# Later transposes of the query numerators, earlier transposes of h, and a last output product in two column parts

## Chip, cores and metric

The kernel runs on one core of one Trainium2 chip. The metric is the device time in microseconds of one execution; lower is better. TensorE (PE, with its weight loads as PEld), VectorE (DVE), ScalarE (ACT), GpSimd (POOL) and SyncE (SP, which here only issues DMAs) each run their own instruction stream in order and wait for one another through semaphores.

## What is computed

The input x has 2048 tokens of 448 features. Both branches start from its layer norm and share one output:

```python
xn = layernorm(x)
# A: linear attention, 16 heads of 28; phi(t) = [softmax(t), softmax(-t)] over 28 features
q, k, v = split(xn @ wqkv)
pq, pk = q @ w_phi, k @ w_phi                      # per head
kv = phi(pk).T @ v ;  z = phi(pk).sum(tokens)      # per head
o  = (phi(pq) @ kv) / (phi(pq) @ z + 1e-6)
A  = o @ wo
# B: token shift and MLP
h  = gelu(layernorm(xn) @ w1)                      # quarters of h shifted by +1,-1,+2,-2 tokens
x1 = xn + shift(h) @ w2
B  = x1 + gelu(layernorm(x1) @ w3) @ w4            # w3: 448 -> 1792, w4: 1792 -> 448
out = x + A + B
```

## The kernel before

Tokens are cut into 16 tiles of 128, in four groups g of four tiles. A small recorder (`Recorder`) takes every operation in program order, finds its hazards by byte ranges, and gives each engine its own in-order stream with the waits that are needed. So the place of a call in the program sets its place in its engine's stream, and nothing else reorders work. All compute calls go through one-line helpers, which is why the profile shows few line numbers: L188 is every matmul, L192 every PE transpose, L196 every activation, L200 every elementwise operation, L203 every DMA transpose, L206 every plain DMA. Tiles of one region show under the region's name or that of its first user: `phik` also holds the MLP's activations h3T, `vaug` also the scratch and output tiles of the late part, `xnT` also o_tok and oT, `w` stands for w1 to w4, `hi` for eqT.

The steps that the change and the prediction touch:

- `q_pair(i, b)`: two tiles of xn @ (wq w_phi) in two PSUM banks; ACT writes exp(+) and exp(-) of them to `eq_tok`, a ring of eight tiles in the region `eq`.
- `eq_T(i)`, in the plan `E`: two DMA transposes on SP of that tile into `eqT`, a ring of eight tiles that fills the region `hi` (16 KB a partition).
- `num_tile(i, b0)`, `N`: 16 matmuls with `eqT` of tile i as weights against `kvq`, then a chain of six operations on DVE (the normaliser) and two on POOL that write `o_tok`. `o_T(i)`, `O`, transposes that by one DMA on SP into `oT`.
- `chunks(n, b)`: 2 of the 56 chunks of x1n @ w3 (14 for each group, 512 tokens wide), with gelu on ACT into h3T. `batch` puts two or more of such pairs together.
- `fin_full(i)`, `Ff`: 14 matmuls with h3T against w4 and 3 with oT against wo, 448 columns each, in one bank; `fin_tail(i)` adds a last half-height matmul; `fin_out(i)` adds x + xn (`x_sum`, on POOL) on DVE into `outb`; `store(i)`, `St`, sends the tile out on SP. For tiles 14 and 15 `fin_full` does all of its four wo matmuls.
- `h_T(i)`: one DMA transpose on SP of a tile of h into hT. `w2_mul(i, b)` needs hT of tiles i-1 to i+1; with `w2_add` (x1 and its statistics, on DVE) it is `W`.
- `ln_scale` on POOL turns the statistics of four tiles of x1 into scales; `g_apply` and `g_T` (`ga`) normalise x1 and transpose it on SP into gT for the chunks of a group.
- `k_norm(i)`: sums and reciprocals on DVE, then a multiplication on POOL (the last tile's on DVE) that normalises phi(pk) in `phik`. `kv_tile(i)`: eight small matmuls with it; after tile 15, `kv_copy` on DVE, `kv_blocks` (8 PE transposes, then DVE) give `kvq`.

Up to tile 3 of `kv_tile` the program is written out; then a list `plan` of nine rows drives it. Each row names the banks of its chunk pairs, which form a batch, and the steps after them in order:

```python
for *heads, steps in plan:
    pairs_b = [chunks(n + 2 * k, b) for k, b in enumerate(heads)]
    n += 2 * len(pairs_b)
    batch(pairs_b[:2], pairs_b[2:], led=held)
    held = [step[1] for step in steps if step[0] is fin_full]
    for step in steps:
        step[0](*step[1:])
```

After the plan come tiles 12 and 13's ends and the last two output products, of tiles 14 and 15.

Of the kernel before, what the change touches and what calls it, by code (L numbers as in the profile page):

```python
# [5 lines left out]
ACT = mybir.ActivationFunctionType  # L6
ALU = mybir.AluOpType
# [201 lines left out]
def bass_parallel_sum__linear_kernel_hedgehog__mixer_s_mlp__prompt_kernel(  # L209
    nc, A_x, A_wqkv, A_w_phi, A_wo, B_x, B_w1, B_w2, B_w3, B_w4, out,  # L210
):
    _, S, D = A_x.shape
# [3 lines left out]
    NT, NG, KC, NC, NM, FC, HP = 16, 4, 4, 4, 4, 14, 32  # L216
    CR = 112
    SHIFTS = [1, -1, 2, -2]
    QE = DH + 2
    PAD = 16  # L220
    HW = S + 2 * PAD
    x2d, out2d = A_x[0], out[0]

    es = ExitStack()
    with es:
        R = Recorder(nc, es)
# [9 lines left out]
        def view(h, cols, dt=BF16, at=0):  # L236
            a = h[:, at // 2:at // 2 + cols * DTB[dt] // 2]
            return a if dt == BF16 else a.bitcast(dt)
# [5 lines left out]
        for b in range(4):  # L244
            t = es.enter_context(nc.psum_tensor("bank%d%d" % (2 * b, 2 * b + 1), [128, 1024], F32))
            R.track(t, 4096, psum=True)
            pairs.append(t)
        banks = [pairs[b // 2][:, 512 * (b % 2):512 * (b % 2) + 512] for b in range(8)]
# [11 lines left out]
        vaug = view(vaug_r, NT * 512).rearrange("p (t c) -> p t c", t=NT)  # L260
        gT = new("gT", 2 * KC * 512).rearrange("p (b c s) -> p b c s", b=2, c=KC)
        eq_r = region("eq", 8 * 2 * 512 * 2)
        eq_tok = view(eq_r, 8 * 2 * 512).rearrange("p (t s d) -> p t s d", t=8, s=2)
        hi_r = region("hi", NC * 2 * 1024 * 2)
        eqT = view(hi_r, 8 * 2 * 512).rearrange("p (t s c f) -> p t s c f", t=8, s=2, c=NC)
        wT = view(hi_r, 2 * NC * 512).rearrange("p (t c d) -> p t c d", t=2, c=NC)
        wv_r = region("wv", KC * D * 2)
        wv = view(wv_r, KC * D).rearrange("p (c d) -> p c d", c=KC)
# [6 lines left out]
        wo = new("wo", KC * D).rearrange("p (c d) -> p c d", c=KC)  # L275
        w3 = new("w3", KC * F).rearrange("p (c f) -> p c f", c=KC)
        w4_r = region("w4", FC * D * 2)
        w4 = view(w4_r, FC * D).rearrange("p (c d) -> p c d", c=FC)
# [12 lines left out]
        mv2 = new("mv2", NT * 8, F32).rearrange("p (t c) -> p t c", t=NT)  # L291
        rs2 = new("rs2", NT * 8, F32).rearrange("p (t c) -> p t c", t=NT)
# [27 lines left out]
        dve, pool = "DVE", "POOL"  # L320
# [97 lines left out]
        def ln_scale(mvt, rst, a, n, neg):  # L418
            R.ew(pool, "tensor_scalar", mvt[:, a:a + n, 2], mvt[:, a:a + n, 1], LN_EPS, 1.0, op0=ALU.add, op1=ALU.mult)
            R.ew(pool, "tensor_tensor", rst[:, a:a + n, 0], mvt[:, a:a + n, 2], mhalf[:, 0:n], op=ALU.pow)  # L420
            if neg:
                R.ew(pool, "tensor_scalar", rst[:, a:a + neg, 1], mvt[:, a:a + neg, 0], -1.0, 0.0, op0=ALU.mult,
                     op1=ALU.add)
# [92 lines left out]

        def q_pair(i, b):
            def out():
                for s in range(2):
                    R.act(eq_tok[:, i % 8:i % 8 + 2, s, :].rearrange("p t (c d) -> p t c d", c=NC)[:, :, :, 0:CR],  # L520
                          two(b)[:, :, 0:D].rearrange("p t (c d) -> p t c d", c=NC), ACT.Exp, scale=1.0 - 2.0 * s)
            return [tok(wpq, i, b), tok(wpq, i + 1, b + 1)], out

        def eq_T(i):
            for s in range(2):
                R.dma_t(eqT[:, i % 8, s, :, :], eq_tok[:, i % 8, s, :])

        def batch(last, first=(), between=(), led=()):
            for p, _ in last:
# [21 lines left out]
        def h_T(i):  # L551
            R.dma_t(hT[:, :, PAD + 128 * i:PAD + 128 * i + 128], h_tok[i])

        def k_norm(i, eng=pool):
            for j in (i, i + 1):
                ph = phik[:, j, :, :].rearrange("p s (h e) -> p (s h) e", e=DH)
                r = j % 4
                R.ew(dve, "tensor_reduce", ksum[:, r, :], ph, axis=AX.X, op=ALU.add)
                R.ew(dve, "reciprocal", rks[:, r, :], ksum[:, r, :])
                R.ew(eng if j % 2 else pool, "tensor_tensor", ph, ph, rks[:, r, :].unsqueeze(2).to_broadcast([128, 2 * H, DH]),  # L560
                     op=ALU.mult)
# [29 lines left out]
        def w2_tile(i, b):  # L591
            w2_mul(i, b)
            w2_add(i, b)
# [23 lines left out]
        def num_tile(i, b0):  # L617
            g, j = divmod(i, 4)
            r = i % 2
            bs = [banks[b0], banks[b0 + 1]]  # L620
            for s in range(2):
                for c in range(NC):
                    R.mm(bs[s][:, 4 * QE * c:4 * QE * c + 4 * QE], eqT[0:CR, i % 8, s, c, :],
                         kvq[0:CR, 2 * c + s, :], True, True)
            pp, pm = (b[:, 0:H * QE].rearrange("p (h e) -> p h e", e=QE) for b in bs)
            rcpm, rho, dsum, rden = (q_s[:, r, 16 * k:16 * k + 16] for k in range(4))
            R.ew(dve, "reciprocal", rcpm, pm[:, :, DH + 1])
            R.ew(dve, "tensor_tensor", rho, pp[:, :, DH + 1], rcpm, op=ALU.mult)
            R.ew(dve, "tensor_tensor", q_t[:, r, :, :], pm[:, :, 0:DH + 1],
                 rho.unsqueeze(2).to_broadcast([128, H, DH + 1]), op=ALU.mult)  # L630
            R.ew(dve, "tensor_tensor", q_n[:, r, :, :], pp[:, :, 0:DH + 1], q_t[:, r, :, :], op=ALU.add)
            R.ew(dve, "scalar_tensor_tensor", dsum, pp[:, :, DH + 1], DEN_EPS, q_n[:, r, :, DH],
                 op0=ALU.mult, op1=ALU.add)
            R.ew(dve, "reciprocal", rden, dsum)

            cut = 10 if i % 2 else 7
            for h0, h1, at in ((0, cut, 0), (cut - 1, H, 64)):
                R.ew(pool, "tensor_tensor",
                     o_tok[:, i % 4, DH * h0 + at:DH * h1 + at].rearrange("p (h e) -> p h e", e=DH),
                     q_n[:, r, h0:h1, 0:DH], rden[:, h0:h1].unsqueeze(2).to_broadcast([128, h1 - h0, DH]), op=ALU.mult)  # L640
            if i >= NT - 2:
                c0 = 192 + 64 * (i % 2)
                R.ew(pool, "memset", o_tok[:, i % 4, c0:c0 + 64], 0.0)
# [16 lines left out]
        def x_sum(i):  # L660
            R.ew(pool, "tensor_tensor", xs[:, i % 2, :], xn[:, i, 0:D], xtok[:, i, :], op=ALU.add)

        def fin_bank(i):
            return (0 if i > 13 else 4) + i % 2

        def fin_full(i):
            g, j = divmod(i, 4)
            b = banks[fin_bank(i)]
            x_sum(i)
            for fc in range(FC):  # L670
                R.mm(b[:, 0:D], h3T[:, g % 2, fc, 128 * j:128 * j + 128], w4[:, fc, :], fc == 0, False)
            for kc in (0, 3, 2 - i % 2, 1 + i % 2) if i >= NT - 2 else (0, 3, 2 - i % 2):
                R.mm(b[:, 0:D], oT[:, g % 2, kc, 128 * j:128 * j + 128], wo[:, kc, :], False, kc == 1 + i % 2)

        def fin_tail(i):
            g, j = divmod(i, 4)
# [148 lines left out]
        w2_tile(5, 7)  # L825
        qs(4)
        h_T(11)
        for i in range(4, 8):
            eq_T(i)
        k_norm(8)  # L830
        w2_tile(6, 6)
        ks(12)
        w2_tile(7, 7)
        k_norm(10)
        k_norm(12)
        ln_scale(mv2, rs2, 4, 4, 4)
        k_norm(14, dve)
        table("gelu_apprx_tanh_and_others")
        for i in range(4):
# [10 lines left out]
                g_apply(4 * g + j, eng)  # L850
                g_T(4 * g + j)

        def hts():
            for i in range(12, 16):
                h_T(i)
            load_lap(wo, A_wo)

        def sc(g):
# [9 lines left out]
        def stats2(i):  # L868
# [1 line left out]

        plan = [
            (0, 2, 6, [(kv, 4, 8), (load_w4,)]),
            (0, 2, 6, [(table, "exp_and_others"), (ga, 1, dve), (hts,), (qq, 8), (kv, 8, 16), (kv_copy,), (W, 8, 6),
                       (qq, 12), (table, "gelu_apprx_tanh_and_others"), (kv_blocks, 5), (w2_mul, 9, 7), (w2_mul, 10, 6),
                       (w2_add, 9, 7, False), (N, 0, 4), (O, 0), (w2_add, 10, 6, False), (stats2, 9), (stats2, 10), (E, 8)]),
            (0, 2, 4, 6, [(N, 1, 0), (O, 1), (E, 9), (Ff, 0), (W, 11, 3), (sc, 2), (N, 2, 0), (O, 2), (N, 3, 6), (O, 3),
                          (Ff, 1)]),
            (0, 2, 6, [(Ff, 2), (St, 0), (ga, 2), (W, 12, 2), (N, 4, 0), (O, 4), (N, 5, 6), (O, 5), (E, 10), (W, 13, 3), (Ff, 3),
                       (St, 1), (E, 11), (E, 12), (E, 13)]),
            (0, 2, 6, [(Ff, 4), (St, 2), (W, 14, 2), (W, 15, 3), (sc, 3), (N, 6, 0), (O, 6), (N, 7, 6), (O, 7),  # L880
                       (Ff, 5), (St, 3), (ga, 3)]),
            (0, 2, 6, [(Ff, 6), (St, 4), (N, 8, 0), (O, 8), (N, 9, 6), (O, 9), (E, 14), (Ff, 7), (St, 5), (E, 15)]),
            (0, 2, 6, [(Ff, 8), (St, 6), (N, 10, 0), (O, 10), (N, 11, 6), (O, 11), (Ff, 9), (St, 7)]),
            (0, 2, 6, [(Ff, 10), (St, 8), (N, 12, 0), (O, 12), (N, 13, 6), (O, 13), (Ff, 11), (St, 9)]),
            (0, 2, 6, [(N, 14, 0), (O, 14), (Ff, 12), (St, 10), (N, 15, 2), (O, 15), (Ff, 13), (St, 11)])]
        held = []
        n = 0
# [13 lines left out]
        fin_full(14)  # L901
        fin_out(14)
        store(14)
        fin_full(15)
        for h in range(2):
            c = slice(224 * h, 224 * h + 224)
            R.ew(dve, "tensor_tensor", outb[:, 3, c], banks[fin_bank(15)][:, c], xs[:, 1, c], op=ALU.add)
            R.dma(out2d[128 * 15:, c], outb[:, 3, c], "ACT" if h else "SP")

        R.emit()  # L910

# [27 lines left out]
```

## Time and profile before

| | us |
|---|---|
| median of 3 runs | 182.85 (182.31, 182.85, 183.42) |
| the profiled execution, whole | 182.53 |
| its span, first to last instruction | 180.8 |
| PE busy in the span | 175.3 |
| DVE busy | 117.6 |
| POOL busy | 94.6 |
| ACT busy | 80.2 |

The granted TensorE clock was full throughout. Rows of a profile read as follows. In the timeline: start, duration, engine, source line, operation, output<-inputs, partitions x elements, count, and in brackets the idle time of that engine just before and who ended it; several like instructions in a row are merged. In a group: busy time, then the mean duration of one in ns, then idle time before it. A row for SPq or ACTq is an engine's queue issuing a DMA, not the transfer; a DMA group's last number is the median from issue to landing.

### The profile page before, as it was taken

What the parts mean: (1) busy time and instruction counts of PE and PEld (TensorE: products, weight loads), DVE (VectorE), ACT (ScalarE), POOL (GpSimd) and SP (SyncE); (2) the same over time, 40 slices, a digit from 0 to 9 for tenths busy, and PEclk for the clock granted to TensorE, in tenths of its full rate; (3) what the DMA queues carried; (4) which work ended last, traced back from release to release, by engine and by line L of the source; (5) the groups of instructions that cost most, each with busy time, mean ns of one, the idle gap of its engine ahead of it and who ended that gap; (6) DMA issues with size and microseconds to landing.
All of it is one profiled execution on the core that took longest, in us unless ns stands there. A gap on an engine that the chain in (4) does not pass through costs nothing.

```text
span 180.8 us, 3146 instructions
## 1 busy us (share of the span) xinstructions
PE 175.3 (97%) x1200; PEld 88.4 (49%) x1200; DVE 117.6 (65%) x269; ACT 80.2 (44%) x99; POOL 94.6 (52%) x144
## 2 busy tenths in 40 slices
PE   7799999999999999999999999999999999999993
PEld 5454655454445435454553644553644644635551
DVE  5898679659999996874595196195282352654621
ACT  2378881799999639677104104203306006024000
POOL 6874582068999599002457626037835063151650
PEclk9999999999999999999999999999999999999999
DMA  5996445499565499684643323555543422030231
GB/s 165 346 220 128 90 89 102 82 337 232 104 74 110 93 276 229 126 107 70 179 87 62 88 57 64 115 82 112 112 94 80 100 67 80 0 62 25 54 112 44
DMA packets 59142, 21.04 MB, mean 116 GB/s; under 512 B 50872, under 2 KB 58616, under 8 KB 59128
## 3 DMA queue, kind: packets, MB, share of 16 engines
q1 hardware_dynamic: 55656, 16.55, 44.5%
q10 hardware_dynamic: 3472, 4.30, 7.8%
q8 instruction: 9, 0.15, 0.4%
q14 instruction: 5, 0.04, 0.1%
HBM read 7.08 MB, written 1.84 MB: 49 GB/s over the span
## 4 chain that ended last, share of the span: by engine, by line
PE 74%; DVE 16%; POOL 6%; issue 2%; ACT 0%; DVEq 0%
PE bank L188 72%; DVE ksum L200 6%; POOL phik L200 5%; DVE st L200 3%; DVE xn L200 2%; PE bank L192 2%; DVE vaug L200 2%; DVE rks L200 1%; POOL rs L200 1%; POOL mv L200 1%; DVE wpq L200 1%; DVE mv L200 1%; ACT xnT L196 0%; DVEq L166 0%; DVE gT L200 0%
## 5 line engine op out<-in xcount | busy, mean ns | idle before, releaser
L196 ACT ACTIVATE phik<-bank 128x1024 bf16<-128x1024 f32 (+1 forms) x44 | 40.2, 990 | 68.1 <-PE bank L188 68.0
L188 PE MATMUL bank<-gT,w 128*128 128x512 bf16 (+1 forms) x224 | 46.1, 379 | 0.1
L188 PE MATMUL bank<-w,phik 128*128 128x448 bf16 x224 | 45.0, 352 | 0.0
L200 DVE TENSOR_TENSOR vaug<-bank,vaug 128x464 f32<-128x464 f32 (+3 forms) x65 | 33.0, 514 | 17.8 <-PE bank L188 13.9
L200 POOL TENSOR_TENSOR xnT<-vaug 128x196 bf16<-128x196 f32 (+1 forms) x32 | 18.1, 586 | 48.1 <-DVE vaug L200 48.1
L188 PEld LDWEIGHTS bank<-w,phik 128*128 128x128 bf16 x224 | 21.5, 98 | 19.3 <-issue 0.2
L188 PEld LDWEIGHTS bank<-gT,w 128*128 128x128 bf16 (+1 forms) x224 | 17.9, 97 | 24.0 <-issue 5.1
L200 POOL TENSOR_TENSOR phik<-phik,rks 128x896 bf16<-128x896 bf16 x15 | 25.0, 1697 | 3.1 <-DVE rks L200 3.0
L200 POOL TENSOR_TENSOR vaug<-xn,xtok 128x448 f32<-128x448 bf16 x16 | 16.4, 1031 | 1.4 <-DVE vaug L200 1.4
L200 DVE TENSOR_TENSOR xn<-bank,xn 128x448 bf16<-128x448 f32 x16 | 9.4, 599 | 11.8 <-PE bank L188 11.7
L200 DVE TENSOR_REDUCE ksum<-phik 128x32 f32<-128x896 bf16 x16 | 16.6, 1036 | 0.0
L200 DVE RECIPROCAL vaug<-bank 128x16 f32<-128x16 f32 x16 | 3.7, 228 | 17.8 <-PE bank L188 17.8
L188 PE MATMUL bank<-wo,xnT 128*128 128x448 bf16 (+1 forms) x64 | 14.5, 354 | 0.1
L200 POOL TENSOR_TENSOR rs<-mv,mhalf 128x2 f32<-128x2 f32 (+1 forms) x16 | 13.8, 865 | 1.3
L188 PE MATMUL bank<-w,hT 112*128 112x448 bf16 x64 | 14.3, 352 | 0.0
L196 ACT ACTIVATE eq<-bank 128x896 bf16<-128x896 f32 x16 | 13.4, 922 | 1.9 <-PE bank L188 1.9
L188 PE MATMUL bank<-wv,xnT 128*128 128x448 bf16 (+1 forms) x64 | 14.0, 354 | 0.1
L188 PE MATMUL bank<-w,xnT 128*128 128x448 bf16 (+1 forms) x64 | 13.9, 352 | 0.0
L188 PE MATMUL bank<-wpk,xnT 128*128 128x448 bf16 (+1 forms) x64 | 12.2, 353 | 0.0
L188 PE MATMUL bank<-wpq,xnT 128*128 128x448 bf16 (+1 forms) x64 | 12.1, 353 | 0.0
L200 POOL TENSOR_SCALAR mv<-mv 128x4 f32<-128x4 f32 x4 | 1.6, 406 | 17.8 <-DVE mv L200 17.7
L200 DVE BATCH_NORM_STATS2 st<-xn 128x6 f32<-128x448 bf16 x16 | 9.9, 620 | 0.4
(65 smaller groups left out, 173.9 us busy)
## 6 DMA issues: line engine op xcount, KB each, us to landing
w<-in_B_w_dram ACTq DMA_DIRECT2D x2, 896.0 KB, 6.5
out_dram<-vaug SPq DMA_DIRECT2D x15, 112.0 KB, 1.9
w<-in_B_w_dram ACTq DMA_DIRECT2D x1, 1568.0 KB, 9.3
xtok<-in_A_x_dram SPq DMA_DIRECT2D x2, 448.0 KB, 6.6
hi<-eq SPq DMA_TRANSPOSE x32, 2.5
wo<-in_A_wo_dram SPq DMA_DIRECT2D x2, 224.0 KB, 2.9
w<-in_B_w_dram SPq DMA_DIRECT2D x1, 392.0 KB, 4.3
xtok<-in_A_x_dram SPq DMA_DIRECT2D x3, 112.0 KB, 2.6
```

Source lines behind the costliest of these rows:

```text
L188: self.op("PE", lambda e: e.matmul(out, lhsT, rhs, start=start, stop=stop, skip_group_check=True), [out], [lhsT, rhs])
L192: self.op("PE", lambda e: e.transpose(out, in_, ident), [out], [in_, ident])
L196: self.op("ACT", lambda e: e.activation(out, in_, func, **kw), [out], [in_] + aps)
L200: self.op(eng, lambda e: getattr(e, name)(out, *args, **kw), [out], aps)
```

## The change

The eight-slot `eqT` becomes a ring of four, in the lower half of `hi`. The upper half goes to `eq_tok`, which becomes a ring of twelve. `eq_T(i + 4)` now follows `num_tile(i)` in the plan, since it overwrites the slot that `num_tile(i)` has read; before, tiles 4 to 7 were transposed ahead of the plan, and tiles 8 to 15 at other places of it. `h_T` of tiles 12 to 15 moves from the plan's second row to a place ahead of the plan. In that second row the w2 product of tile 8 moves ahead of the kv products of tiles 8 to 15. `ln_scale` for tiles 4 to 7 moves ahead of `k_norm(10)`. The output product of tile 15 is done as 256 columns in one bank and then 192 in another, each with its own addition and store, where before one product of 448 columns was followed by two additions and stores of 224.

```diff
-        eq_tok = view(eq_r, 8 * 2 * 512).rearrange("p (t s d) -> p t s d", t=8, s=2)
-        eqT = view(hi_r, 8 * 2 * 512).rearrange("p (t s c f) -> p t s c f", t=8, s=2, c=NC)
+        eqT = view(hi_r, 4 * 2 * 512).rearrange("p (t s c f) -> p t s c f", t=4, s=2, c=NC)
+        eq_tok = [view(r, 1024, at=at + 2048 * k).rearrange("p (s d) -> p s d", s=2)
+                  for r, at, n in ((eq_r, 0, 8), (hi_r, 8192, 4)) for k in range(n)]
...
         def eq_T(i):
             for s in range(2):
-                R.dma_t(eqT[:, i % 8, s, :, :], eq_tok[:, i % 8, s, :])
+                R.dma_t(eqT[:, i % 4, s, :, :], eq_tok[i % 12][:, s, :])
...
+        def product(i, b, c):
+            g, j = divmod(i, 4)
+            s = slice(128 * j, 128 * j + 128)
+            o = b[:, 0:c.stop - c.start]
+            for fc in range(FC):
+                R.mm(o, h3T[:, g % 2, fc, s], w4[:, fc, c], fc == 0, False)
+            for kc in (0, 3, 2 - i % 2, 1 + i % 2) if i >= NT - 2 else (0, 3, 2 - i % 2):
+                R.mm(o, oT[:, g % 2, kc, s], wo[:, kc, c], False, kc == 1 + i % 2)
+
         def fin_full(i):
...
+            product(i, banks[fin_bank(i)], slice(0, D))
...
         h_T(11)
-        for i in range(4, 8):
-            eq_T(i)
         k_norm(8)
         w2_tile(6, 6)
         ks(12)
         w2_tile(7, 7)
+        ln_scale(mv2, rs2, 4, 4, 4)
         k_norm(10)
+        for i in range(12, 16):
+            h_T(i)
         k_norm(12)
-        ln_scale(mv2, rs2, 4, 4, 4)
         k_norm(14, dve)
...
-        def hts():
-            for i in range(12, 16):
-                h_T(i)
+        def load_wo():
             load_lap(wo, A_wo)
...
         plan = [
             (0, 2, 6, [(kv, 4, 8), (load_w4,)]),
-            (0, 2, 6, [(table, "exp_and_others"), (ga, 1, dve), (hts,), (qq, 8), (kv, 8, 16), (kv_copy,), (W, 8, 6),
+            (0, 2, 6, [(table, "exp_and_others"), (ga, 1, dve), (load_wo,), (qq, 8), (W, 8, 6), (kv, 8, 16), (kv_copy,),
                        (qq, 12), (table, "gelu_apprx_tanh_and_others"), (kv_blocks, 5), (w2_mul, 9, 7), (w2_mul, 10, 6),
-                       (w2_add, 9, 7, False), (N, 0, 4), (O, 0), (w2_add, 10, 6, False), (stats2, 9), (stats2, 10), (E, 8)]),
-            (0, 2, 4, 6, [(N, 1, 0), (O, 1), (E, 9), (Ff, 0), (W, 11, 3), (sc, 2), (N, 2, 0), (O, 2), (N, 3, 6), (O, 3),
+                       (w2_add, 9, 7, False), (N, 0, 4), (E, 4), (O, 0), (w2_add, 10, 6, False), (stats2, 9), (stats2, 10),
+                      ]),
+            (0, 2, 4, 6, [(N, 1, 0), (E, 5), (O, 1), (Ff, 0), (W, 11, 3), (sc, 2), (N, 2, 0), (E, 6), (O, 2), (N, 3, 6), (E, 7), (O, 3),
                           (Ff, 1)]),
-            (0, 2, 6, [(Ff, 2), (St, 0), (ga, 2), (W, 12, 2), (N, 4, 0), (O, 4), (N, 5, 6), (O, 5), (E, 10), (W, 13, 3), (Ff, 3),
-                       (St, 1), (E, 11), (E, 12), (E, 13)]),
-            (0, 2, 6, [(Ff, 4), (St, 2), (W, 14, 2), (W, 15, 3), (sc, 3), (N, 6, 0), (O, 6), (N, 7, 6), (O, 7),
+            (0, 2, 6, [(Ff, 2), (St, 0), (ga, 2), (W, 12, 2), (N, 4, 0), (E, 8), (O, 4), (N, 5, 6), (E, 9), (O, 5), (W, 13, 3), (Ff, 3),
+                       (St, 1),]),
+            (0, 2, 6, [(Ff, 4), (St, 2), (W, 14, 2), (W, 15, 3), (sc, 3), (N, 6, 0), (E, 10), (O, 6), (N, 7, 6), (E, 11), (O, 7),
                        (Ff, 5), (St, 3), (ga, 3)]),
-            (0, 2, 6, [(Ff, 6), (St, 4), (N, 8, 0), (O, 8), (N, 9, 6), (O, 9), (E, 14), (Ff, 7), (St, 5), (E, 15)]),
-            (0, 2, 6, [(Ff, 8), (St, 6), (N, 10, 0), (O, 10), (N, 11, 6), (O, 11), (Ff, 9), (St, 7)]),
+            (0, 2, 6, [(Ff, 6), (St, 4), (N, 8, 0), (E, 12), (O, 8), (N, 9, 6), (E, 13), (O, 9), (Ff, 7), (St, 5),]),
+            (0, 2, 6, [(Ff, 8), (St, 6), (N, 10, 0), (E, 14), (O, 10), (N, 11, 6), (E, 15), (O, 11), (Ff, 9), (St, 7)]),
...
-        fin_full(15)
-        for h in range(2):
-            c = slice(224 * h, 224 * h + 224)
-            R.ew(dve, "tensor_tensor", outb[:, 3, c], banks[fin_bank(15)][:, c], xs[:, 1, c], op=ALU.add)
-            R.dma(out2d[128 * 15:, c], outb[:, 3, c], "ACT" if h else "SP")
+        x_sum(15)
+        for c, b, e in ((slice(0, 256), 1, "SP"), (slice(256, D), 2, "ACT")):
+            product(15, banks[b], c)
+            R.ew(dve, "tensor_tensor", outb[:, 3, c], banks[b][:, 0:c.stop - c.start], xs[:, 1, c], op=ALU.add)
+            R.dma(out2d[128 * 15:, c], outb[:, 3, c], e)
```

More of the change, by code (lines that the diff above doesn't have):

```diff
@@ L518, in out @@
             def out():
+                r, at = (eq_r, i % 12) if i % 12 < 8 else (hi_r, 4 + i % 12 - 8)
+                e = view(r, 2048, at=2048 * at).rearrange("p (t s c d) -> p t s c d", t=2, s=2, c=NC)
                 for s in range(2):
-                    R.act(eq_tok[:, i % 8:i % 8 + 2, s, :].rearrange("p t (c d) -> p t c d", c=NC)[:, :, :, 0:CR],
+                    R.act(e[:, :, s, :, 0:CR],
                           two(b)[:, :, 0:D].rearrange("p t (c d) -> p t c d", c=NC), ACT.Exp, scale=1.0 - 2.0 * s)
@@ L622, in num_tile @@
                 for c in range(NC):
-                    R.mm(bs[s][:, 4 * QE * c:4 * QE * c + 4 * QE], eqT[0:CR, i % 8, s, c, :],
+                    R.mm(bs[s][:, 4 * QE * c:4 * QE * c + 4 * QE], eqT[0:CR, i % 4, s, c, :],
                          kvq[0:CR, 2 * c + s, :], True, True)
@@ L664, in fin_bank @@
             return (0 if i > 13 else 4) + i % 2
+        def product(i, b, c):
[6 more added lines that the diff above has]
+                R.mm(o, oT[:, g % 2, kc, s], wo[:, kc, c], False, kc == 1 + i % 2)
         def fin_full(i):
-            g, j = divmod(i, 4)
-            b = banks[fin_bank(i)]
             x_sum(i)
[L670 to L673, printed above, removed]
+            product(i, banks[fin_bank(i)], slice(0, D))
         def fin_tail(i):
```

## Prediction

> **What bounds the kernel.** I read the page's busy times first, then the chain that ended last, then the timeline of PE around each place where that chain leaves PE. The page:
>
> ```profile
> PE 175.3 (97%) x1200; PEld 88.4 (49%) x1200; DVE 117.6 (65%) x269; ACT 80.2 (44%) x99; POOL 94.6 (52%) x144
> ```
>
> PE is busy for 97% of the span; the others have a third of it free or more. So a change that leaves PE's matmuls as they are can only win time where PE waits, and after PE's last matmul. The chain shows two such waits in the stretch that is edited:
>
> ```profile
> 70.94 1.66 POOL phik L200
> 72.60 0.04 issue
> ...
> 88.67 0.08 issue
> ...
> ```
>
> At 72.60 PE comes back from a POOL multiplication into phik (`k_norm` of tile 14). At 88.67 it comes back from something that no engine did. An idle time that the profile shows after a drained pipeline understates the loss, since the next matmul's start no longer overlaps the last one's end; so I take the loss from start to start, against the same sequence where it doesn't wait. PE's timeline (start, duration; `phik,vaug` are the kv products, `w,phik` the w4 product, `wo,xnT` its wo part, `kvq,hi` the numerators):
>
> ```profile
> 62.36 0.98 PE L188 MATMUL bank<-phik,vaug 128*64 128x112 bf16 x32
> 63.27 4.92 PE L188 MATMUL bank<-gT,w 128*128 128x512 bf16 x24
> ...
> 70.98 1.37 PE L188 MATMUL bank<-phik,vaug 128*64 128x112 bf16 x48
> 72.65 0.58 PE L188 MATMUL bank<-phik,vaug 128*64 128x112 bf16 x16 [0.29 <-POOL phik L200]
> 73.16 0.93 PE L188 MATMUL bank<-w,hT 112*128 112x448 bf16 x4
> ...
> 85.86 2.81 PE L188 MATMUL bank<-w,phik 128*128 128x448 bf16 x14
> 88.75 0.73 PE L188 MATMUL bank<-wo,xnT 128*128 128x448 bf16 x3
> ...
> 90.07 1.00 PE L188 MATMUL bank<-kvq,hi 112*128 112x120 bf16 x16
> 90.91 2.81 PE L188 MATMUL bank<-w,phik 128*128 128x448 bf16 x14
> 93.56 0.73 PE L188 MATMUL bank<-wo,xnT 128*128 128x448 bf16 x3
> ```
>
> First wait: 64 kv products take 73.16 - 70.98 = 2.18 us. Undisturbed, 32 take 63.27 - 62.36 = 0.91, so 64 take 1.82 and the loss is 0.36. With the 16 that take 73.16 - 72.65 = 0.51 as a second point, one costs 25 ns and a start 0.11: then 64 take 1.71 and the loss is 0.47. I take 0.40. Second wait: 14 w4 matmuls take 88.75 - 85.86 = 2.89 for tile 0 and 93.56 - 90.91 = 2.65 for tile 1: a loss of 0.24.
>
> **First part: the kv products no longer wait.** Two edits act here. The rows around them:
>
> ```profile
> 60.16 0.18 DVE L200 BATCH_NORM_AGGREGATE mv<-st 128x2 f32<-128x6 f32 x1
> 61.78 6.66 POOL L200 TENSOR_TENSOR phik<-phik,rks 128x896 bf16<-128x896 bf16 x4 [2.08 <-DVE rks L200]
> 68.54 1.02 POOL L200 TENSOR_SCALAR mv<-mv 128x4 f32<-128x4 f32 x1
> 70.57 3.35 ACT L196 ACTIVATE eq<-bank 128x896 bf16<-128x896 f32 x4
> 70.98 2.74 DVE L200 TENSOR_SCALAR g_tok<-xn,mv,rs 128x512 bf16<-128x512 bf16 x4 [1.48 <-POOL rs L200]
> 73.63 1.25 DVE L200 CAST wpk<-bank 64x448 bf16<-64x448 f32 x2
> 76.79 0.61 PE L192 MATMUL bank<-ident,wpk 128*112 128x128 bf16 x8
> 77.44 1.19 DVE L200 TENSOR_TENSOR kvq<-bank,maskb 112x464 bf16<-112x464 bf16 x2 [1.02 <-PE bank L192]
> 78.75 0.58 PE L188 MATMUL bank<-kvq,hi 112*128 112x120 bf16 x8
> ```
>
> `ln_scale` for tiles 4 to 7 sits on POOL from 68.54 to 70.94 between four and one multiplications of `k_norm`. It moves in front of them. Its input, the statistics of tile 7, is there at 60.34 (60.16 + 0.18), while POOL idles for 2.08 us until 61.78. Run from 60.34 at the full 2.40, it ends at 62.74 and delays the four by 0.96; they end at 69.5 and the fifth, 1.66 long, at 71.2 where it ended at 72.6. That is the bad end: most of it lies in the idle time. PE meanwhile does the w2 product of tile 8 at 70.98 (at most 0.93), and reaches tile 14 of the kv products 48 matmuls after 71.9, at 73.1. Nothing waits: 1.9 us of cover, and without it the old loss is back.
>
> What the new order queues behind what: on DVE, `g_apply` no longer waits 1.48 us for POOL and runs from 69.5 to 72.2. Then W(8) comes ahead of `kv_copy`. In the profile W(8) fills DVE from 74.88 (73.63 + 1.25) to 76.42 (77.44 - 1.02), 1.54 us; now it does so from 72.2 to 73.8, `kv_copy` ends at 75.0, and PE needs it for the eight transposes at 76.79 less the 0.4 gained: 1.4 us of cover. The second `qq` finds its first two banks free, since ACT leaves them halfway through the run of four from 70.57, at 72.2. `kvq` and the numerators of tile 0 at 78.75 keep their distance to these transposes and come 0.4 sooner too. Gain 0.40.
>
> **Second part: the SP queue, and the wait of tile 0's product.** The rows:
>
> ```profile
> 60.93 11.69 SPq L203 DMA_TRANSPOSE hi<-eq  x8
> ...
> 81.77 1.13 POOL L200 TENSOR_TENSOR xnT<-vaug 128x196 bf16<-128x196 f32 x2 [9.18 <-DVE vaug L200]
> ...
> 85.35 1.19 SPq L203 DMA_TRANSPOSE xnT<-xnT  x1
> ```
>
> POOL has `o_tok` of tile 0 at 82.90, but SP issues its transpose only at 85.35. Eight transposes of `eq_T` held SP to 72.62, and behind them stood four of gT, four of h and the loads of wo. With 2.5 us to land (row below) O(0) is there at 87.8 to 88; PE wanted it at 88.51. The 0.08 of idle with no engine named fits this. In the new order, h's four transposes take the place of the eight at 60.93, so gT and wo are issued early, and `eq_T(4)` goes out after N(0) ends, at 79.3, takes 2.57 and is off SP by 81.9, before POOL is done. O(0) is issued at 82.9 less 0.4 and lands 2.4 us sooner than before. Gain 0.24; of h, tile 12 is first needed by W(11), behind the product of tile 0, so its move costs nothing.
>
> The new waits stand on SP: `eq_T(i+4)` waits for PE's N(i), and O(i) stands behind it. O(i) has to wait for DVE and POOL after the same N(i) anyway, 3.6 us in tile 0. So one pair is covered. In each later row there are two pairs for two O's, and the second pair stands behind the first O. The tightest place is tiles 8 and 9, where the four gT of the last group come first:
>
> ```profile
> hi<-eq SPq DMA_TRANSPOSE x32, 2.5
> ...
> 90.85 2.57 SPq L203 DMA_TRANSPOSE hi<-eq  x2
> ...
> 127.32 5.13 SPq L203 DMA_TRANSPOSE gT<-g_tok  x4
> 132.49 0.58 SPq L206 DMA_DIRECT2D out_dram<-vaug  x1
> ...
> 141.63 0.73 PE L188 MATMUL bank<-wo,xnT 128*128 128x448 bf16 x3
> ...
> 145.69 0.73 PE L188 MATMUL bank<-wo,xnT 128*128 128x448 bf16 x3
> ```
>
> In the old clock, at the latest: gT ends at 132.45, plus 2.57 for E(11) ahead of it, 0.6 for the store, 2.57 for E(12): O(8) is issued at 138.2 and lands at 140.7, where PE uses it at 141.63. O(9) follows 1.2 + 2.57 later, at 142.0, and lands at 144.5 before 145.69. Margins 0.9 and 1.2; I charge nothing, and leave the overrun to a rival. Numerators read `eqT` a row after its transposes, with several us to spare.
>
> **Third part: the end.**
>
> ```profile
> 171.42 1.19 SPq L203 DMA_TRANSPOSE xnT<-xnT  x1
> ...
> 174.49 2.81 PE L188 MATMUL bank<-w,phik 128*128 128x448 bf16 x14
> ...
> 177.13 0.92 PE L188 MATMUL bank<-wo,xnT 128*128 128x448 bf16 x4
> 178.09 0.69 DVE L200 TENSOR_TENSOR vaug<-bank,vaug 128x224 bf16<-128x224 f32 x2 [2.78 <-PE bank L188]
> 178.81 0.37 ACTq L206 DMA_DIRECT2D out_dram<-vaug  x1
> ```
> ```profile
> L188 PEld LDWEIGHTS bank<-kvq,hi 112*128 112x128 bf16 x128 | 7.6, 98 | 1.9
> ...
> L200 DVE TENSOR_TENSOR vaug<-bank,vaug 128x224 bf16<-128x224 f32 x2 | 0.7, 386 | 2.8 <-PE bank L188 2.8
> ```
>
> Before, two additions stand in a row after the last matmul, 178.09 to 178.78, and then the second store. After, only the addition of 192 columns does: 0.35, between 0.386 x 192/224 = 0.33 and 0.386. The 18 matmuls become 36 over the same columns. Their spacing is 2.65 / 14 = 189 ns at 448 columns and (90.91 - 90.07) / 16 = 52.5 ns at 120, so 0.417 ns a column plus 2.5 ns each: 82 ns at 192 columns, and 18 more of them cost 0.045. The end comes at 178.48 instead of 178.78: a gain of 0.30 (0.26 to 0.35). The first part's addition and store lie beside the second part's matmuls. Tile 15's wo matmuls start 1.1 us sooner, at about 176.0; their transpose, issued at 171.42, lands at 173.9.
>
> What could spoil this is the weight loads, which double. One lasts 98 ns, longer than 82. But the numerators load as many columns every 52.5 ns, so loads overlap; bounds for the narrow half's spacing are 82 and 98 ns, and I take 82 because the nearest row is narrower still. The Trainium skill speaks against the change here (TensorE: Matmul & The Clock Gate, section LDWEIGHTS (loading the stationary operand)): a load takes its columns divided by 1.2 in ns, so 107 for 128, an estimate by which 18 loads end to end would add 0.45 us to the narrow half and turn the end into a loss of 0.15. The trace agrees with that as the duration of one load, and not as the spacing.
>
> **Sum.** 0.40 + 0.24 + 0.30 = 0.94 us. The profiled execution took 182.53 (span 180.8): 181.6 after, span 179.9. The median of the three runs lies 0.32 above that execution: 182.85 - 0.94 = **181.9**.
>
> **Rivals.**
> *Weight loads bound the narrow half.* At 98 ns each 18 of them cost 0.29 more, the end gains nothing, and 0.65 is left: 182.2. For: 98 exceeds 82, and no row has a 192-column matmul. Against: the 52.5 ns. 16%.
> *SP falls behind, and PE waits for O(8) or O(9): slower.* From E(11) to O(9) SP has twelve transposes. At 1.46 each (11.69 / 8) instead of 1.28 they end 2.15 us later, 0.95 past the margin of 1.2, and the gain is just gone: 182.9. At 1.6 each they end 3.85 later and PE waits 2.65: 184.6. Slower by over the bound below it is from 1.54 each. For: the run of eight shows more than 1.28 for a while. Against: that run shared the DMA engines with the load of w4, and my clock here counts nothing that moved out of the way (before, three pairs stood ahead of O(6)). 9%, of which 8 over the bound of slower.
> *The change doesn't reach the first wait* (another input of the kv products was last, not POOL's): 0.54 is left, 182.3. The bracket at 72.65 names POOL phik, so 5%.
> *More than forecast*: the first wait's larger loss, 0.47, with 0.24 and the end's 0.35: 1.06, 181.8. 4%.
>
> **Numbers.** The forecast has 66%. A measurement of this kernel tells about 0.5%, 0.91 us, from no change, and the forecast's 0.94 sits on that line: the sizes put 45 of the 66 over it and 21 under. Faster 45 + 4 = 0.49; slower 0.08; the rest 0.43. For the range I take 181.8 with the runs' scatter of about 0.55 (182.31 to 183.42) below, and the weight loads' 182.2 with the same scatter above: 181.2 to 182.8.
>
> **What would show it.** Right: no bracket of POOL phik at the kv products and W(8) in front of them; `ln_scale`'s rows near 60.4; 14 w4 matmuls of tile 0 in 2.65; O(0) issued near 82.5; one DVE addition of about 0.35 after the last matmul; the narrow half's 18 matmuls in about 1.5. Wrong: those 18 in 1.8 or more; PE idle before the wo matmuls of tiles 8 to 11 with SP's DMA as the releaser; DVE's `kv_copy` after 76; a new bracket at the second `qq`.

## The result: about 1 us less

| | before | changed |
|---|---|---|
| median of 11 executions, us | 182.52 | 181.59 |
| range, us | 182.17 to 183.42 | 181.34 to 182.26 |
| profiled execution, us | 182.53 | 181.43 |
| its span, us | 180.8 | 179.7 |

The two medians differ by 0.93 us. The ratio of changed to before is 0.9942 (95%: 0.9924 to 0.9959), which is 1.06 us (0.75 to 1.39) of 182.52. The forecast was 0.94 us and 181.9. Two executions of the kernel no_sp below, at 184.36 and 185.72, lie more than 1.5% above its fastest and are left out of its ratio.

The page of the changed kernel, busy times and the chain's shares:

```profile
PE 175.9 (98%) x1218; PEld 90.5 (50%) x1218; DVE 117.6 (65%) x269; ACT 80.2 (45%) x99; POOL 94.6 (53%) x144
...
PE 95%; DVE 3%; ACT 0%; issue 0%
```

The work of DVE, ACT and POOL is what it was; PE has 18 matmuls more. POOL has left the chain that ended last. PE's timeline at the places that the prediction named:

```profile
70.71 0.92 PE L188 MATMUL bank<-w,hT 112*128 112x448 bf16 x4
71.56 1.76 PE L188 MATMUL bank<-phik,vaug 128*64 128x112 bf16 x64
73.26 3.03 PE L188 MATMUL bank<-wpq,xnT 128*128 128x448 bf16 x16
...
85.19 2.81 PE L188 MATMUL bank<-w,phik 128*128 128x448 bf16 x14
87.84 0.73 PE L188 MATMUL bank<-wo,xnT 128*128 128x448 bf16 x3
```

W(8) stands first, the 64 kv products follow in one row without a bracket and take 73.26 - 71.56 = 1.70 us (2.18 before). The 14 w4 matmuls of tile 0 take 87.84 - 85.19 = 2.65 (2.89 before). What should have freed them, in the timeline of all engines:

```profile
60.25 0.20 POOL L200 TENSOR_SCALAR mv<-mv 128x4 f32<-128x4 f32 x1 [0.73 <-DVE mv L200]
...
61.80 9.17 POOL L200 TENSOR_TENSOR phik<-phik,rks 128x896 bf16<-128x896 bf16 x5
...
73.41 1.22 DVE L200 CAST wpk<-bank 64x448 bf16<-64x448 f32 x2
...
82.27 1.19 SPq L203 DMA_TRANSPOSE xnT<-xnT  x1
```

`ln_scale` fills 60.25 to 61.84, in POOL's old idle time, and the five multiplications of `k_norm` run through to 70.97. `kv_copy` ends at 74.63, ahead of the transposes at 76.13. O(0) is issued at 82.27 instead of 85.35. The end:

```profile
175.67 1.32 PE L188 MATMUL bank<-w,phik 128*128 128x192 bf16 x14
175.87 0.42 DVE L200 TENSOR_TENSOR vaug<-bank,vaug 128x256 bf16<-128x256 f32 x1 [1.34 <-PE bank L188]
176.83 0.49 PE L188 MATMUL bank<-wo,xnT 128*128 128x192 bf16 x4
177.36 0.36 DVE L200 TENSOR_TENSOR vaug<-bank,vaug 128x192 bf16<-128x192 f32 x1 [1.06 <-PE bank L188]
177.75 0.36 ACTq L206 DMA_DIRECT2D out_dram<-vaug  x1
```

One addition of 0.36 is left behind the last matmul. The narrow matmuls are spaced (176.83 - 175.67) / 14 = 83 ns. One new wait has come, at tile 8:

```profile
138.07 2.81 PE L188 MATMUL bank<-w,phik 128*128 128x448 bf16 x14
140.84 0.30 PEld L188 LDWEIGHTS bank<-wo,xnT 128*128 128x128 bf16 x3 [0.39 <-DMA xnT<-xnT]
```

There the 14 w4 matmuls take 2.77 until 140.84 instead of 2.65, and a DMA, O(8), is named. The two profiled spans add up: PE starts the first kv products 0.18 us sooner (62.18 against 62.36), in a stretch that no edit touches; then 0.49 at the kv products (0.48 in the products, 0.01 around them), 0.24 at O(0), -0.12 at O(8), and 0.28 behind tile 14's product (from its wo part to the last store's issue: 177.75 - 172.95 = 4.80 against 178.81 - 173.73 = 5.08). That is 1.07 of 1.1, and the edits account for 0.89 of it.

### The profile page after: what moved, and what is told of

It reads as the page before. It is cut to its first block, busy times and chain, and to the rows that moved or that the text cites. A ratio compares the mean times of both kernels' runs of the same rounds, so it can differ in the third digit from the quotient of the medians.

```text
span 179.7 us, 3181 instructions
## 1 busy us (share of the span) xinstructions
PE 175.9 (98%) x1218; PEld 90.5 (50%) x1218; DVE 117.6 (65%) x269; ACT 80.2 (45%) x99; POOL 94.6 (53%) x144
## 3 DMA queue, kind: packets, MB, share of 16 engines
HBM read 7.08 MB, written 1.84 MB: 50 GB/s over the span
## 4 chain that ended last, share of the span: by engine, by line
PE 95%; DVE 3%; ACT 0%; issue 0%
PE bank L188 93%; PE bank L192 2%; DVE vaug L200 1%; DVE st L200 1%; DVE xn L200 1%; ACT xnT L196 0%; DVE mv L200 0%; DVE gT L200 0%
## 5 line engine op out<-in xcount | busy, mean ns | idle before, releaser
L188 PE MATMUL bank<-w,phik 128*128 128x448 bf16 (+2 forms) x238 | 45.2, 342 | 0.0
L188 PEld LDWEIGHTS bank<-w,phik 128*128 128x128 bf16 x238 | 22.6, 98 | 18.4 <-issue 0.2
L200 POOL TENSOR_TENSOR phik<-phik,rks 128x896 bf16<-128x896 bf16 x15 | 25.8, 1754 | 1.0 <-DVE rks L200 0.9
L188 PE MATMUL bank<-wo,xnT 128*128 128x448 bf16 (+3 forms) x68 | 14.7, 344 | 0.0
L196 ACT ACTIVATE eq<-bank 128x896 bf16<-128x896 f32 x12 | 10.0, 923 | 1.4 <-PE bank L188 1.4
L200 POOL TENSOR_SCALAR mv<-mv 128x4 f32<-128x4 f32 x4 | 0.8, 203 | 18.2 <-DVE mv L200 18.2
L200 DVE BATCH_NORM_STATS2 st<-xtok 128x6 f32<-128x448 bf16 x16 | 9.8, 612 | 0.8 <-DMA xtok<-in_A_x_dram 0.7
```

The lines of the kernel that those rows point to most:

```text
L188: self.op("PE", lambda e: e.matmul(out, lhsT, rhs, start=start, stop=stop, skip_group_check=True), [out], [lhsT, rhs])
L196: self.op("ACT", lambda e: e.activation(out, in_, func, **kw), [out], [in_] + aps)
L200: self.op(eng, lambda e: getattr(e, name)(out, *args, **kw), [out], aps)
```

## One part at a time

Each kernel is timed beside runs of the kernel before on the same chip; their medians there were 183.06, 183.11 and 183.17, with single executions between 182.3 and 184.8, so higher and more scattered than the 182.52 above. Differences of 0.1 us are read from traces, not from medians.

**scale_only**: before, with `ln_scale` moved.

```diff
         w2_tile(7, 7)
+        ln_scale(mv2, rs2, 4, 4, 4)
         k_norm(10)
         k_norm(12)
-        ln_scale(mv2, rs2, 4, 4, 4)
```

> The kernel before with one edit: ln_scale for tiles 4 to 7 ahead of k_norm(10). Theory (the first wait is POOL's multiplication for tile 14, late only because ln_scale stands in front of it): POOL's fifth multiplication ends by 71.2 instead of 72.6, PE reaches tile 14 at 72.3, so the bracket is gone, the 64 kv products take about 1.70 us instead of 2.18, and the time falls by 0.4 to 0.5 us (ratio 0.997 to 0.998). Rival (another input of the kv products was last): they still take about 2.18 and the time stays. The late O(0) and its 0.24 stay in both.

182.92 us, ratio 0.9991 (0.9968 to 1.0015). PE's timeline, first the kv products, then tile 0:

```profile
70.97 1.76 PE L188 MATMUL bank<-phik,vaug 128*64 128x112 bf16 x64
72.67 0.93 PE L188 MATMUL bank<-w,hT 112*128 112x448 bf16 x4
```

The products take 1.70: the wait was POOL's, and this edit alone ends it. But the time didn't follow. In the same profile the 14 w4 matmuls of tile 0 run from 85.36 to a wo part at 89.30: 3.94 instead of 2.89. In this execution O(0) takes back what the kv products won, and more: PE comes 0.5 us sooner (85.36 against 85.86), and O(0) is issued 0.5 later (85.85 against 85.35).

**w_only**: before, with W(8) moved.

```diff
-  ... (qq, 8), (kv, 8, 16), (kv_copy,), (W, 8, 6), ...
+  ... (qq, 8), (W, 8, 6), (kv, 8, 16), (kv_copy,), ...
```

> The kernel before with one edit: the w2 product of tile 8 ahead of the kv products of tiles 8 to 15. Theory: PE reaches tile 14 only at about 73.05, after POOL's end at 72.6, so the kv products take 1.70 here too and no bracket is left; but DVE, whose g_apply still waits for ln_scale and ends at 73.7, now does W(8) until 75.2 and kv_copy until 76.5, while PE wants kv_copy at 76.3: about 0.2 to 0.4 us of a new PE wait at the eight transposes, so a gain of 0.1 to 0.3 us. Rival (W's place alone is as good as both edits): a gain of 0.45 and no wait at the transposes.

182.88 us, ratio 1.0 (0.9976 to 1.0024). Its PE rows:

```profile
71.92 1.76 PE L188 MATMUL bank<-phik,vaug 128*64 128x112 bf16 x64
73.62 3.04 PE L188 MATMUL bank<-wpq,xnT 128*128 128x448 bf16 x16
76.50 0.65 PE L192 MATMUL bank<-ident,wpk 128*112 128x128 bf16 x8
...
78.93 1.46 PE L188 MATMUL bank<-gT,w 128*128 128x512 bf16 x6
81.05 5.12 PE L188 MATMUL bank<-gT,w 128*128 128x512 bf16 x26 [0.67 <-DMA gT<-g_tok]
86.01 0.59 PE L188 MATMUL bank<-kvq,hi 112*128 112x120 bf16 x8
86.43 2.81 PE L188 MATMUL bank<-w,phik 128*128 128x448 bf16 x14
90.24 0.73 PE L188 MATMUL bank<-wo,xnT 128*128 128x448 bf16 x3 [0.99 <-DMA xnT<-xnT]
```

The kv wait is gone here too, and the expected wait at the transposes hardly came: `kv_copy` ended at 76.45, just as PE wanted it (76.50 - 73.62 = 2.88 against 2.86). That detail was missed. What ate the gain in this execution is again SP: the chunk batch of the third row waits for gT and takes 86.01 - 78.93 = 7.08 instead of 6.26, and tile 0's w4 matmuls take 3.81.

**sp_only**: the changed kernel without the POOL edit, the W edit and the new product; only the rings, the places of the transposes and of the wo loads. **o0_first**: the kernel before, with one edit on SP alone.

```diff
-            for i in range(12, 16):
-                h_T(i)
+            h_T(12)
             load_lap(wo, A_wo)
...
-  ... (O, 0), (w2_add, 10, 6, False), ...
+  ... (O, 0), (h_T, 13), (h_T, 14), (h_T, 15), (w2_add, 10, 6, False), ...
```

> The changed kernel without its POOL edit, without its W edit and with the old last product: only the rings, the places of the transposes of q and h, and of the loads of wo. Theory: the kv products still take about 2.18 us; O(0) is issued as soon as POOL is done and the 14 w4 matmuls of tile 0 take 2.65 instead of 2.89, a gain of 0.24; O(8) lands late as in the changed kernel, 14 w4 matmuls of tile 8 take 2.77 instead of 2.65, a loss of 0.12. Together 0.1 to 0.2 us faster than before (ratio about 0.999). Rival (O(0) was late for another reason than the queue): no gain, a loss of 0.1.

> The kernel before with one edit: h's transposes of tiles 13 to 15 behind O(0) on SP instead of ahead of it (tile 12 and wo stay ahead). It takes three transposes, 4 us, from what stands before O(0), and leaves POOL, PE and the end as they are. Theory A: O(0) is issued near 82.9, the 14 w4 matmuls of tile 0 take 2.65 in every execution, the kernel gains 0.2 to 0.6 us against before by the median and its runs scatter less (before: 182.4 to 184.1), since this wait is what varies. Rival (the scatter has another source): the same scatter as before, and a gain of 0.24 or less.

sp_only: 182.52 us, ratio 0.9983 (0.9964 to 1.0002). o0_first: 182.63 us, ratio 0.9966 (0.9943 to 0.9989), executions between 182.29 and 183.35, against 182.27 to 184.63 of before beside it. In both the kv products still wait, and in both tile 0 doesn't. The rows of o0_first:

```profile
72.75 0.58 PE L188 MATMUL bank<-phik,vaug 128*64 128x112 bf16 x16 [0.30 <-POOL phik L200]
...
85.95 2.81 PE L188 MATMUL bank<-w,phik 128*128 128x448 bf16 x14
88.61 0.73 PE L188 MATMUL bank<-wo,xnT 128*128 128x448 bf16 x3
```
```profile
83.03 1.20 SPq L203 DMA_TRANSPOSE xnT<-xnT  x1
```

Three transposes less ahead of O(0) and it goes out at 83.03, with 88.61 - 85.95 = 2.66 on PE. It also lands sooner after its issue, in 2.4 us. In the first profile of before it took 3.3:

```profile
DMA to landing us min/median/max: 3.3/3.3/3.3
```

Issued at 85.35, it was there at 88.6, 0.1 after PE wanted it (85.86 + 2.65 = 88.51). In all six profiles with the old order O(0) stands directly behind the two loads of wo and takes 3.1 to 3.3 us; in all others it doesn't stand there and takes 2.4. That the loads are the reason fits this, but no run tests it alone.

The order of one queue is worth 0.54 us by the medians and 0.6 by the ratio (0.2 to 1.0 by the interval), against 0.24 in the first profile. The executions spread over 1.1 us in twelve, those of before over 2.4 in 23; those of sp_only spread over 1.7, by a single one at 183.93. So much of the scatter goes with the order; that all of it does isn't shown. In sp_only PE didn't wait for O(8), against what was expected: PE and O(8)'s issue both come 0.7 us later than in the changed kernel, but O(8) lands in 4.0 us instead of 4.3, at 141.25, and PE wants it at 141.44.

**no_sp**: the changed kernel without its SP part. **before_again**: the kernel before, profiled once more.

> The changed kernel without its SP part: rings of eight, the transposes of q and h and the loads of wo where they were; the POOL edit, the W edit and the new last product stay. Theory A (O(0)'s landing is set by the SP queue, full since about 37 us, and not by PE, so what PE gains ahead of it is given back there): the kv products take 1.70 us, but the 14 w4 matmuls of tile 0 take 2.65 plus the old 0.24 plus the 0.49 gained, 3.4 or more (3.94 and 3.81 were seen with one edit); in all only the end's 0.3 us is left, ratio 0.998. Theory B of the prediction (the three gains add up): 2.89 there, and 0.7 to 0.8 us faster than before, ratio 0.996.

> The kernel before, unchanged, for a second profile. Theory A: kv products 2.18 us and the end as in the first profile, but the 14 w4 matmuls of tile 0 take another time than 2.89, as O(0) is issued and lands at another time; 2.74, 3.81 and 3.94 were seen in kernels that share its queue. Rival: 2.89 again.

no_sp: 183.09 us, ratio 0.9985 (0.9953 to 1.0017), executions from 181.59 to 185.72. PE in its third row, then the same rows of before_again (184.52 us):

```profile
78.81 1.46 PE L188 MATMUL bank<-gT,w 128*128 128x512 bf16 x6
80.63 5.12 PE L188 MATMUL bank<-gT,w 128*128 128x512 bf16 x26 [0.36 <-DMA gT<-g_tok]
85.59 0.58 PE L188 MATMUL bank<-kvq,hi 112*128 112x120 bf16 x8
86.01 2.81 PE L188 MATMUL bank<-w,phik 128*128 128x448 bf16 x14
90.28 0.73 PE L188 MATMUL bank<-wo,xnT 128*128 128x448 bf16 x3 [1.45 <-DMA xnT<-xnT]
```
```profile
79.69 1.46 PE L188 MATMUL bank<-gT,w 128*128 128x512 bf16 x6
82.68 5.12 PE L188 MATMUL bank<-gT,w 128*128 128x512 bf16 x26 [1.52 <-issue]
87.63 0.58 PE L188 MATMUL bank<-kvq,hi 112*128 112x120 bf16 x8
88.06 2.81 PE L188 MATMUL bank<-w,phik 128*128 128x448 bf16 x14
90.70 0.73 PE L188 MATMUL bank<-wo,xnT 128*128 128x448 bf16 x3
```

The unchanged kernel lost 87.63 - 79.69 = 7.94 less 6.26, so 1.68 us, at the batch, and nothing at tile 0, where its first profile lost 0 and 0.24. Its SP queue, in the timeline of SP alone, and the landing of its four gT:

```profile
60.51 1.27 SPq L203 DMA_TRANSPOSE hT<-w  x1
61.83 12.30 SPq L203 DMA_TRANSPOSE hi<-eq  x8
74.17 5.20 SPq L203 DMA_TRANSPOSE gT<-g_tok  x4
79.41 3.74 SPq L203 DMA_TRANSPOSE hT<-h  x2
```
```profile
DMA to landing us min/median/max: 2.5/2.5/4.5
```

The queue has no gap from 60.51 on. Eight transposes took 12.30 here and 11.69 in the first profile, and gT starts at 74.17 instead of 72.77. That alone would have cost nothing: the last gT is issued at 78.11, and with the usual 2.5 us to land it would have been there at 80.6, while PE's first six matmuls last until 79.69 + 1.46 = 81.15. It took 4.5 us, to 82.59, and PE goes on at 82.68. The issue right behind it was a long one: two transposes of h took 3.74 us where 2.58 is usual.

In the first profile the same thing happened a little later in the queue: two transposes of h took 3.60 us from 80.56. Without that extra 1.0 us O(0) would have been issued at 84.3 and, with its 3.3 to land, been there at 87.6, before the 88.51 at which PE wanted it (an estimate from these rows). So in both profiles of before, by this reckoning, the loss took two things: a queue that is full ahead of gT and O(0), and one long issue in it. Where that issue fell decided what was late. The other four kernels with the old order have one too, 3.45 to 3.73 us for two transposes of h ahead of O(0). The changed kernel has one as well (E(4), from 78.50, takes 3.11 instead of 2.57), but there nothing waits for it. The losses at the batch and at tile 0, side by side (undisturbed: 6.26 and 2.65):

| kernel | chunk batch of the third row, us | 14 w4 matmuls of tile 0, us | lost, us |
|---|---|---|---|
| before, first profile | 6.26 | 2.89 | 0.24 |
| before, second profile | 7.94 | 2.64 | 1.68 |
| tail_only | 6.26 | 2.74 | 0.09 |
| scale_only | 6.26 | 3.94 | 1.29 |
| w_only | 7.08 | 3.81 | 1.98 |
| no_sp | 6.78 | 4.27 | 2.14 |
| sp_only, o0_first, no_w, changed | 6.26 | 2.65 | 0.00 |

Each of these profiles with the old order loses here, by another amount each time; none with the new order does. In the trace of no_sp the gains ahead of O(0) are given back: its kv products take 1.70 (71.86 to 73.56), and 2.14 is lost behind them. Its times say less. The ratio of 0.9985 has 1 in its interval, but also the 0.996 of three gains that add up; over all twelve executions its mean is 183.18, that of before 183.21. And in some executions the gain stays: three of the twelve took 181.59, 181.79 and 182.01, all below the fastest of 23 of before beside them, 182.27.

**no_w**: the changed kernel with W(8) back behind the kv products.

> The changed kernel with the w2 product of tile 8 back behind the kv products. Theory (POOL's fifth multiplication ends by about 71 with ln_scale ahead of the four, and PE reaches tile 14 at 72.2): no wait comes back, the kv products take 1.70 us and the time is that of the changed kernel within 0.1 us. Rival (both edits are needed): part of the old 0.49 us is back and POOL phik has a bracket.

181.67 us, ratio 0.9919 (0.9892 to 0.9946). The rows:

```profile
71.24 1.76 PE L188 MATMUL bank<-phik,vaug 128*64 128x112 bf16 x64
72.94 0.93 PE L188 MATMUL bank<-w,hT 112*128 112x448 bf16 x4
```

1.70 us and no bracket: W's new place adds nothing to this once `ln_scale` has moved.

**tail_only**: before, with the last product in 256 and 192 columns. **tail_384**: the changed kernel, cut at 384 instead of 256.

> The kernel before with the last product in 256 and 192 columns and nothing else. Theory (only the second addition of 0.39 leaves the end): spacing about 83 ns in the narrow half, DVE's last addition 0.36, the span's end 0.3 us sooner behind PE's last w4 run of tile 14 than before (ratio 0.998 to 0.9985). Rival (weight loads of 98 ns bound the narrow half): 18 matmuls in 1.76 and no gain.

> The changed kernel with its last product cut at 384 columns, so that the narrow part has 64. It asks where weight loads would bind. If loads of 128 columns overlap at any rate, the 18 narrow matmuls are spaced 0.417 x 64 + 2.5 = 29 ns, 0.5 us in all, PE's end stays, DVE's last addition takes about 0.22 instead of 0.36, and the end is 0.14 sooner. If the array can't take loads faster than about the 52.5 ns seen at 120 columns, the 18 take 0.95 us, PE ends 0.4 later and the kernel loses 0.25 to 0.3 us against the cut at 256. If loads bound at their 98 ns: 1.76 us, and it loses 1.1.

tail_only: 182.54 us, ratio 0.998 (0.9955 to 1.0005). From tile 14's wo part to the last store's issue it takes 178.44 - 173.64 = 4.80, as in the changed kernel, against 5.08 before. tail_384: 181.89 us, ratio 0.992 (0.9887 to 0.9953). Its narrow matmuls:

```profile
176.68 0.57 PE L188 MATMUL bank<-w,phik 128*128 128x64 bf16 x14
...
177.09 0.28 PE L188 MATMUL bank<-wo,xnT 128*128 128x64 bf16 x4
```

(177.09 - 176.68) / 14 = 29 ns a matmul, each with its own load of 128 columns: even at 64 columns, loads of 98 ns don't set the spacing. Its store is issued 4.66 behind tile 14's wo part, 0.14 sooner than in the changed kernel, as expected; the median, 181.89 beside 181.59, doesn't show it.

**late_e**: the changed kernel with E(12) and E(13) behind O(8) and O(9). **swap_banks**: with the chunk pairs of the sixth row in banks 2, 0, 6. **best**: both, and a cut at 320.

```diff
-            (0, 2, 6, [(Ff, 6), (St, 4), (N, 8, 0), (E, 12), (O, 8), (N, 9, 6), (E, 13), (O, 9), (Ff, 7), (St, 5),]),
+            (2, 0, 6, [(Ff, 6), (St, 4), (N, 8, 0), (O, 8), (N, 9, 6), (O, 9), (E, 12), (E, 13), (Ff, 7), (St, 5),]),
...
-        for c, b, e in ((slice(0, 256), 1, "SP"), (slice(256, D), 2, "ACT")):
+        for c, b, e in ((slice(0, 320), 1, "SP"), (slice(320, D), 2, "ACT")):
```

> The changed kernel with the transposes E(12) and E(13) behind O(8) and O(9) instead of each behind its N. Theory (PE's wait before the wo part of tile 8 comes from SP's backlog: four gT, a store and E(12) ahead of O(8)): O(8) is issued near 134 instead of 136.5 and lands by 136.5, the 14 w4 matmuls of tile 8 take 2.65 instead of 2.77, a gain of 0.12 us (ratio to the changed kernel 0.9993), and no bracket with a DMA is left. Rival (the long landing of 4.3 us belongs to that moment and not to the backlog): O(8) still lands 4 us after its issue, but with 2.5 us more room PE waits for nothing either; then the landing time, not the wait, tells them apart.

> The changed kernel with the first two chunk pairs of the sixth plan row in exchanged banks (2, 0, 6 instead of 0, 2, 6). Theory (PE's wait at 120.9, 0.52 us of idle weight load, is for DVE to finish reading the numerators of tile 6 in banks 0 and 1, after the additions and statistics of tiles 14 and 15): banks 2 and 3 are free by then, banks 0 and 1 are wanted 1.28 us later, so the wo part of tile 5 to the first chunk takes 0.57 instead of 0.82 and the kernel gains 0.25 us (ratio 0.9986 to the changed kernel). Rival (PE would wait for DVE at the next pair instead): the 0.25 turns up 1.28 us later.

> The changed kernel with late_e's order, swap_banks' banks and a last product of 320 and 128 columns. Theory (the three waits are independent): 0.12 + 0.25 + about 0.07 for a shorter last addition, since 128 columns at 0.417 x 128 + 2.5 = 56 ns are still above the 52.5 seen: 0.44 us less than the changed kernel, about 181.15 against 181.6 (ratio to before 0.992). If the last part is bound by weight loads, 0.2 less of that.

late_e: 181.59 us, 0.99 (0.9862 to 0.9938). swap_banks: 181.67 us, 0.9904 (0.9871 to 0.9938). best: 181.44 us (181.15 to 182.16), 0.9897 (0.9854 to 0.994). SP in the changed kernel, and its O(8) from issue to landing; then the same two in late_e:

```profile
136.52 1.26 SPq L203 DMA_TRANSPOSE xnT<-xnT  x1
137.83 3.47 SPq L203 DMA_TRANSPOSE hi<-eq  x2
```
```profile
DMA to landing us min/median/max: 4.3/4.3/4.3
```
```profile
134.33 2.64 SPq L203 DMA_TRANSPOSE xnT<-xnT  x2
137.01 6.37 SPq L203 DMA_TRANSPOSE hi<-eq  x4
```
```profile
DMA to landing us min/median/max: 2.4/2.4/2.5
```

In late_e O(8) goes out at 134.33 and lands in 2.4; PE takes 2.65 at tile 8. The place behind gT, the store and E(12) did not cost the 0.12 alone: issued at 136.52 and landing in 2.4, O(8) would have been there at 138.9, and PE wanted it at 138.07 + 2.65 = 140.72. The 4.3 of its landing made it late. The landing time was to tell theory and rival apart and can't, since in late_e O(8) also leaves at another moment; the transpose of `eq` that goes out at 137.01 in its stead lands after 4.3. So the late landing stayed where it was, and late_e moved O(8) out of its way. More on it below.

swap_banks ends the wait at 120.9: from tile 5's wo part (120.39) to the end of the first 12 chunk matmuls (123.64) it takes 3.25 instead of 123.61 - 120.10 = 3.51. But it arrives 0.26 sooner at O(8) and waits there:

```profile
138.10 2.81 PE L188 MATMUL bank<-w,phik 128*128 128x448 bf16 x14
141.08 0.74 PE L188 MATMUL bank<-wo,xnT 128*128 128x448 bf16 x3 [0.17 <-DMA xnT<-xnT]
```

2.98 instead of 2.77: 0.21 given back, the same trade as in scale_only. best has neither wait. From its first kv products at 62.40 to its last store's issue at 177.51 it takes 115.11, the changed kernel 177.75 - 62.18 = 115.57: 0.46 less in one trace of each, where 0.44 was worked out. The medians, 181.44 beside 181.59, agree in sign and can't resolve it.

## Why the prediction was right, and where it was not

*First part, 0.40.* It measured 0.48 to 0.49: the second of the two prices (25 ns a product and 0.11 for a start), 0.47, was right to 0.02. The reason, POOL's multiplication behind `ln_scale`, is shown by scale_only. "Two edits act here" was too generous: no_w shows that the W edit isn't needed, and w_only that either is enough to end this wait. The end of the fifth multiplication came out near the forecast, 70.97 for 71.2, but by other sizes: `ln_scale` took 1.6 us and not 2.4, and the multiplications 1.83 each (9.17 / 5) and not 1.67.

*Second part, 0.24.* The mechanism, O(0) behind a full SP queue, is shown by sp_only and o0_first. One step of its working doesn't hold: with 2.5 us to land O(0) is there at 87.8 to 88, and that is before the 88.51 at which PE wanted it, so by these numbers PE would not have waited. O(0) took 3.3 us and came at 88.6. The other step that failed is the size: 0.24 was what one execution lost. The second profile of the same kernel lost 1.68, and kernels that share its queue between 0.09 and 2.14. The prediction took the queue's state at 60.93 as given and didn't ask how often a long issue falls into it, or where. It fits this that beside later runs of before, with medians 0.6 us higher, the new order stands at 0.990 to 0.992 and not at 0.994; that the queue is the reason for that shift isn't shown.

*The sum.* Adding the first and second part was right only because both edits are made. What is gained ahead of O(0) stays for certain only if the queue ahead of it is short; the trace of no_sp shows the three parts not adding up.

*Charging nothing to the tightest place, O(8).* Wrong by 0.12. O(8) was issued earlier than the bound (136.52 against 138.2 less the 0.9 gained), but landed in 4.3 us where the median, 2.5, was taken. The rival named the right place, by another cause (the pace of twelve transposes) and at a price far above what it cost.

*The end, 0.30.* It measured 0.28. *Weight loads*, the likeliest rival: fell. 83 ns at 192 columns and 29 at 64, with loads of 98 ns. The Trainium skill's duration for a load (TensorE: Matmul & The Clock Gate, section LDWEIGHTS (loading the stationary operand)) agrees with the trace within 9 ns, 107 against 98; taken as a bound on spacing, which the section doesn't call it, it would have been wrong by a factor of 3.7 at 64 columns. The same page of the Trainium skill, section Back-to-back issue gap, gives N/2.4 + 2.5 ns, 29.2 and 82.5 here, and warns that with few columns a stream with loads is slower, 81 ns at 128 columns; the first agrees with the trace, the second doesn't (55.7 at 128 columns in best: 14 matmuls from 175.98 to 176.76).

*The numbers.* 181.59 lies in 181.2 to 182.8, and the medians' 0.93 meets the 0.94. The level, 181.9, was 0.3 too high, since the median of three runs that it started from, 182.85, stood that much above the median of eleven, 182.52. The gain was met partly by luck: 0.12 was lost at O(8), and 0.09 more than forecast was won at the kv products.

## What to carry to other kernels

A queue that issues in order, without a gap for tens of us, is a second path beside the busiest engine: compute what it is late by, from issues and landings and in more than one execution, before any gain ahead of it is counted. Where an engine's gain vanishes, look at the next wait for a transfer; here a POOL edit worth 0.48 us on PE gave no time that twelve runs could show until the queue was shortened. And a scatter of 2 us between executions of one kernel may come from such a queue, which a trace of the fastest execution hardly shows.

## What the hardware showed besides

Now and then SP needs 2.0 to 2.6 us for issuing a DMA transpose instead of 1.3. Near 80 us the six profiles with the old order have one such issue (2.1 to 2.4 us), and the transpose before it lands after 4.1 to 4.5; near 138 us the changed kernel and the six variants of it with the new transposes have one (2.0 to 2.6 us). In every kernel with E(12) ahead of O(8) the latter is the one right behind O(8) (137.83 above: two in 3.47 us), and O(8) lands after 4.0 to 4.4 us; in late_e and best the same position in the queue falls to a transpose of `eq`, and O(8) lands after 2.4. So it doesn't belong to the tile. In all seven it is SP's 100th DMA, but it also comes at nearly the same time, 137.8 to 138.5 us. In the kernel before it is the 104th, at 138.9 in one profile and 140.8 in the other, and near 80 us the 64th in one and the 62nd in the other. Whether a count or a moment sets it, and why it comes, is open.
